# Landings of the GpSimd load queue modelled one microsecond later in a kernel's planner, and a new order of work

## The chip, the cores and the metric

The kernel runs on one core of one Trainium2 chip. The metric is the device time of one execution in microseconds (us); less is better. Eight runs of the kernel before took 263.6, 265.0, 262.32, 261.89, 261.75, 263.05, 262.64 and 262.27 us: the median is 262.48 us.

A core has engines that each work through their own list of instructions in order: TensorE (PE in the profile; it multiplies matrices, and loads weights beside that, PEld), VectorE (DVE), ScalarE (ACT), GpSimd (POOL) and SyncE (SP). They wait for each other by semaphores. Transfers from and to memory (DMA) are issued here by two of them: SP, whose queue is q1, and POOL, whose queue is q0. Both queues are served by the same 16 DMA engines.

## What is computed

Attention over selected blocks, and then a mixer of tokens and of channels on its output. Sizes: 4 batches, 8 heads, 768 positions, 64 values per head; 512 channels, 256 hidden tokens, 1536 hidden channels.

```python
k_rep = k.reshape(B, H, n_blocks, block, D).mean(axis=3)          # blocks of 64 positions
gate_scores = np.einsum('bhsd,bhnd->bhsn', q, k_rep)              # causal blocks only
top_idx = np.argsort(gate_scores, axis=-1)[..., -3:]              # three blocks, and the own one
scores = np.where(mask, q @ k.T / np.sqrt(D), -1e9)
x = softmax(scores) @ v                                           # then heads side by side: 512 channels
h = np.maximum(xt @ w_tok1, 0.0) @ w_tok2                         # xt: x with tokens last
u = x + h.transpose(0, 2, 1)
out = u + np.maximum(u @ w_ch1, 0.0) @ w_ch2
```

## The kernel before

**Work.** Heads are handled in 16 pairs, numbered 0 to 15; four pairs make a batch. For each pair i:

- SP loads k and q (`load_qk`, L453; two halves of 192 KB each; three buffers for k and three for q).
- PE turns them (`transposes`, L498; here "turn k i" and "turn q i", six matmuls each) into a PSUM buffer of the ring "big", which has two buffers; ACT or DVE copies the result out (`evac_t`).
- POOL casts it into the 16-bit arrays KA and QA, one half for each head x (`cast`, L513; "cast k i x").
- PE and DVE find the selected blocks (gate, three largest values, mask).
- PE computes scores (`scores`, L672) in three groups for each head, also into "big"; ACT takes the exponential (L685); DVE masks the diagonal (L692).
- PE multiplies with v ("av i x", L704), and DVE normalises. v of pair i is loaded by POOL's queue (`load_v`, L460; "V i"), into one of six buffers.

For each batch the mixer follows: tok1 (L766 in batch 0, L735 after it), umix (L780, L747), ch1 (L816), ch2 (L833), and the store. Its weights come by POOL's queue in ten loads, W0 to W9: W0 and W1 for tok1 and umix, W2 to W5 for ch1, W6 to W9 for ch2.

**Order.** The kernel writes no order by hand. A planner in the kernel (`plan`) runs when the program is built. It gives every piece of work a cost and a priority, plays the engines forward in its own model, and records the pieces in the order of that model; each engine then executes its pieces in just this order. The priorities are base values plus a table of some 500 small corrections, `NUDGE`, which a search found ("climbed") for the model. Two more tables say after which cast a load on POOL's queue may stand: `VAFTER` for V 0 to V 15 and `WAIT` for W0 to W9 (used at L994 to L1002). They set places in POOL's list, and no waits for data.

In the model of the DMA queues (`transfers`) the queue of POOL and that of SP share a rate, and a load counts as landed some time after its last byte: 1200 ns for POOL's queue, 700 ns for SP's. Where the model sees PE idle in the first 46 us, the planner puts small matmuls on a buffer of zeros there (`dummy`, L850, 55 ns each)[...].

Of the kernel before, what the change touches and what calls it, by code (L numbers as in the profile page):

```python
# [40 lines left out]
def QACT(i):  # L41
# [3 lines left out]
VAFTER = [('kt', 1, 1), ('qt', 3, 1), ('qt', 3, 1), ('qt', 3, 1), ('qt', 4, 1), ('qt', 4, 1), ('kt', 7, 1), ('qt', 8,  # L45
    1), ('qt', 10, 1), ('qt', 12, 1), ('qt', 12, 1), ('qt', 12, 1), ('kt', 13, 1), ('qt', 14, 1), ('kt', 14,
    1), ('kt', 12, 1)]
# [4 lines left out]
WAIT = [('kt', 1, 1), ('kt', 1, 1), ('kt', 3, 1), ('kt', 3, 1), ('qt', 4, 1), ('qt', 4, 1), ('kt', 9, 1), ('qt', 6,  # L52
    1), ('qt', 6, 1), ('qt', 10, 1)]


NUDGE = {('av', 0, 0): 1.303, ('av', 0, 1): 19.19, ('av', 1, 0): 3.0, ('av', 1, 1): 7.0, ('av', 10, 0): 12.27, ('av',
    10, 1): -1.3, ('av', 11, 0): 8.583, ('av', 11, 1): 1.7, ('av', 12, 0): -10.583, ('av', 12, 1): -3.759,
    ('av', 13, 0): -9.736, ('av', 13, 1): -13.215, ('av', 14, 0): 9.3, ('av', 14, 1): -6.4, ('av', 15, 0):
    1.5, ('av', 15, 1): -16.1, ('av', 2, 0): -24.676, ('av', 2, 1): -5.771, ('av', 3, 0): -15.21, ('av', 3,
    1): 14.3, ('av', 4, 0): 0.224, ('av', 4, 1): -15.976, ('av', 5, 0): 9.232, ('av', 5, 1): -3.9, ('av', 6,  # L60
    0): 1.19, ('av', 6, 1): 4.4, ('av', 7, 0): 4.184, ('av', 7, 1): 4.895, ('av', 8, 0): -26.172, ('av', 8,
    1): -1.175, ('av', 9, 0): 4.793, ('av', 9, 1): 20.5, ('bias', 0): -9.3, ('bias', 1): -35.4, ('bias', 2):
    -10.876, ('bias', 3): -28.1, ('bias', 4): 5.3, ('bias', 5): -4.817, ('bias', 6): -24.7, ('bias', 7):
    -12.0, ('bias', 8): 1.624, ('cast', 'kt', 0): 7.5, ('cast', 'kt', 1): -14.6, ('cast', 'kt', 10): -7.747,
    ('cast', 'kt', 11): -15.7, ('cast', 'kt', 12): -14.8, ('cast', 'kt', 13): -12.198, ('cast', 'kt', 14):
    -6.8, ('cast', 'kt', 15): -9.29, ('cast', 'kt', 2): 1.0, ('cast', 'kt', 3): 5.0, ('cast', 'kt', 4):
    -13.647, ('cast', 'kt', 5): 18.165, ('cast', 'kt', 6): 33.55, ('cast', 'kt', 7): -14.305, ('cast', 'kt',
    8): 2.4, ('cast', 'kt', 9): 7.4, ('cast', 'qt', 0): 7.252, ('cast', 'qt', 1): 8.4, ('cast', 'qt', 10):
    -8.041, ('cast', 'qt', 11): 5.7, ('cast', 'qt', 12): 1.4, ('cast', 'qt', 13): 7.4, ('cast', 'qt', 14):
    -12.496, ('cast', 'qt', 15): 8.0, ('cast', 'qt', 2): -5.802, ('cast', 'qt', 3): -8.9, ('cast', 'qt', 4):  # L70
    3.916, ('cast', 'qt', 5): 30.7, ('cast', 'qt', 6): -10.2, ('cast', 'qt', 7): 8.8, ('cast', 'qt', 8): -8.4,
    ('cast', 'qt', 9): 1.1, ('ch1', 0, 1): -0.8, ('ch1', 0, 2): 3.2, ('ch1', 0, 3): 2.5, ('ch1', 1, 0): -9.2,
    ('ch1', 1, 1): -11.5, ('ch1', 1, 2): 0.7, ('ch1', 1, 3): 0.5, ('ch1', 2, 1): -3.7, ('ch1', 2, 2): -0.9,
    ('ch1', 2, 3): -10.3, ('ch1', 3, 0): -7.3, ('ch1', 3, 1): -0.4, ('ch1', 3, 2): 0.3, ('ch1', 3, 3): -0.3,
    ('dg', 0, 0): -17.2, ('dg', 0, 1): 2.993, ('dg', 1, 0): -2.7, ('dg', 1, 1): -4.7, ('dg', 10, 0): -13.711,
    ('dg', 10, 1): 6.989, ('dg', 11, 0): 6.4, ('dg', 11, 1): -19.8, ('dg', 12, 0): 2.907, ('dg', 12, 1): 6.1,
    ('dg', 13, 0): -0.81, ('dg', 13, 1): 6.8, ('dg', 14, 0): 20.5, ('dg', 14, 1): -11.389, ('dg', 15, 0):
    21.39, ('dg', 15, 1): 2.9, ('dg', 2, 0): 2.145, ('dg', 2, 1): -3.182, ('dg', 3, 0): 9.793, ('dg', 3, 1):
    -0.1, ('dg', 4, 0): 11.12, ('dg', 4, 1): -0.9, ('dg', 5, 0): -5.9, ('dg', 5, 1): -1.348, ('dg', 6, 0):
    9.4, ('dg', 6, 1): 10.7, ('dg', 7, 0): -11.565, ('dg', 7, 1): 6.3, ('dg', 8, 0): 0.2, ('dg', 8, 1):  # L80
    -6.683, ('dg', 9, 0): 8.793, ('dg', 9, 1): 11.1, ('ex', 1, 0): 8.2, ('ex', 1, 1): 1.7, ('ex', 10, 0):
    -12.228, ('ex', 10, 1): 30.172, ('ex', 11, 0): 11.3, ('ex', 11, 1): 5.059, ('ex', 12, 0): 6.8, ('ex', 12,
    1): -6.9, ('ex', 13, 0): 5.202, ('ex', 13, 1): -16.7, ('ex', 14, 0): 19.3, ('ex', 14, 1): 2.2, ('ex', 15,
    0): 19.9, ('ex', 15, 1): 0.422, ('ex', 2, 0): 4.583, ('ex', 2, 1): -5.641, ('ex', 3, 0): 12.596, ('ex', 3,
    1): 18.909, ('ex', 4, 0): 9.424, ('ex', 4, 1): -7.694, ('ex', 5, 0): 5.485, ('ex', 5, 1): -17.7, ('ex', 6,
    0): -24.1, ('ex', 6, 1): 0.6, ('ex', 7, 0): -23.0, ('ex', 7, 1): -6.974, ('ex', 8, 0): -16.166, ('ex', 8,
    1): 9.077, ('ex', 9, 0): 17.89, ('ex', 9, 1): 5.545, ('gate', 0): 17.0, ('gate', 1): -7.9, ('gate', 11):
    -6.1, ('gate', 15): -10.725, ('gate', 2): 6.749, ('gate', 3): -6.2, ('gate', 4): -1.007, ('gate', 5):
    19.769, ('gate', 7): 2.6, ('gm', 0): 46.696, ('gm', 1): 17.1, ('gm', 2): -5.382, ('gm', 3): -4.582, ('gm',
    4): 18.193, ('gm', 5): 6.763, ('gm', 6): 8.191, ('gm', 7): -1.6, ('gm', 8): -4.431, ('kcopy', 0): 8.403,  # L90
    ('kcopy', 1): -13.1, ('kcopy', 10): -0.34, ('kcopy', 11): 6.362, ('kcopy', 12): 12.117, ('kcopy', 13):
    -3.285, ('kcopy', 14): 5.152, ('kcopy', 15): 1.6, ('kcopy', 2): -0.869, ('kcopy', 3): -3.3, ('kcopy', 4):
    -12.187, ('kcopy', 5): 2.0, ('kcopy', 6): 35.9, ('kcopy', 7): 4.195, ('kcopy', 8): -0.043, ('kcopy', 9):
    6.264, ('ksum', 0): 17.593, ('ksum', 1): 11.0, ('ksum', 10): 17.559, ('ksum', 11): 4.7, ('ksum', 12):
    -4.3, ('ksum', 13): -7.9, ('ksum', 14): -3.033, ('ksum', 15): -3.69, ('ksum', 2): 17.048, ('ksum', 3):
    -2.1, ('ksum', 4): 26.3, ('ksum', 5): 12.754, ('ksum', 6): 1.797, ('ksum', 7): 3.6, ('ksum', 8): -54.4,
    ('kt', 0): 3.4, ('kt', 1): 7.0, ('kt', 10): 11.272, ('kt', 11): 0.8, ('kt', 12): 14.2, ('kt', 13): -9.9,
    ('kt', 14): -13.5, ('kt', 15): 10.118, ('kt', 2): 13.818, ('kt', 3): -22.9, ('kt', 4): -12.776, ('kt', 5):
    -11.008, ('kt', 6): -17.826, ('kt', 7): -33.297, ('kt', 8): -20.826, ('kt', 9): 2.028, ('lt', 0): -25.61,
    ('lt', 1): -5.5, ('lt', 2): 9.2, ('lt', 3): -25.3, ('lt', 4): 0.9, ('lt', 5): -2.1, ('lt', 6): 6.0, ('lt',  # L100
    7): -5.5, ('lt', 8): -10.776, ('mask', 0): 14.19, ('mask', 1): 9.1, ('mask', 2): -5.031, ('mask', 3):
    -2.9, ('mask', 4): -3.463, ('mask', 5): 15.502, ('mask', 6): 2.681, ('mask', 7): 8.708, ('mask', 8):
    -34.0, ('norm', 0, 0): 3.203, ('norm', 0, 1): -5.307, ('norm', 1, 0): 1.7, ('norm', 1, 1): 11.8, ('norm',
    10, 0): -2.676, ('norm', 10, 1): -13.641, ('norm', 11, 0): 24.7, ('norm', 11, 1): -17.9, ('norm', 12, 0):
    -19.1, ('norm', 12, 1): -5.0, ('norm', 13, 0): -2.7, ('norm', 13, 1): -12.84, ('norm', 14, 0): 1.337,
    ('norm', 14, 1): -20.9, ('norm', 15, 0): -1.2, ('norm', 15, 1): -19.577, ('norm', 2, 0): 9.823, ('norm',
    2, 1): -49.782, ('norm', 3, 0): -0.1, ('norm', 3, 1): -21.3, ('norm', 4, 0): 13.385, ('norm', 4, 1): -6.8,
    ('norm', 5, 0): 17.905, ('norm', 5, 1): -5.6, ('norm', 6, 0): 12.08, ('norm', 6, 1): -2.7, ('norm', 7, 0):
    5.72, ('norm', 7, 1): 0.2, ('norm', 8, 0): -17.047, ('norm', 8, 1): -19.759, ('norm', 9, 0): -3.855,
    ('norm', 9, 1): 8.6, ('put', 0): -5.51, ('put', 1): -11.9, ('put', 10): -3.841, ('put', 11): -1.8, ('put',  # L110
    12): -13.5, ('put', 13): -11.209, ('put', 14): 6.6, ('put', 15): 11.1, ('put', 2): 4.118, ('put', 3):
    10.7, ('put', 4): -2.9, ('put', 5): 6.805, ('put', 6): -12.923, ('put', 7): -23.98, ('put', 8): -24.414,
    ('put', 9): 6.5, ('qt', 0): -10.7, ('qt', 1): 8.0, ('qt', 10): -9.6, ('qt', 11): 13.6, ('qt', 12): 23.4,
# [43 lines left out]
             norm=3, tok1=3, relu1=3, uput=3, utr=3, umix=4, uadd=4)  # L157
# [32 lines left out]
def transfers(moves):  # L190
# [4 lines left out]
    now, ends = 0.0, {}  # L195
    while todo[True] or todo[False]:
# [13 lines left out]
        for q, (_, o) in head.items():  # L210
            left[id(o)] -= step * rate[q]
            if left[id(o)] <= 1e-6:
                todo[q].pop(0)
                ends[o] = now + (1200 if q else 700)
# [946 lines left out]
```

## Time and profile before

| what | value |
|---|---|
| median of 8 runs | 262.48 us |
| the profiled execution: its time | 263.6 us |
| its span, from the first to the last instruction | 261.9 us |
| matmuls / DVE / ACT / POOL busy | 253.7 / 159.7 / 144.0 / 78.5 us |
| granted TensorE clock | full in the mean |
| V loads: issue to landing, least / median / most | 4.3 / 6.5 / 12.3 us |
| k loads / q loads: median to landing | 5.1 / 5.7 us |
| weight loads: median to landing | 7.4 us (8 for ch1, ch2), 8.0 us (2 for tok1, umix) |

The spans of matmuls overlap in the profile, since they are pipelined: "busy" says that PE had something in flight. How fast it goes is seen from the distance of starts in an unbroken row. A long row of L833 has 52 matmuls of 512 columns in 11.22 us, that is 0.216 us for each.

### The profile page before, as it was taken

To read this page: it belongs to the slowest core of one execution; us is meant where nothing else is said; L and a number is where in the kernel's file an instruction comes from. 1 tells how busy PE (TensorE), PEld (TensorE's weight loads), DVE (VectorE), ACT (ScalarE), POOL (GpSimd) and SP (SyncE) were. 2 spreads that over 40 slices of the span, in tenths; PEclk is the share of its full clock that TensorE was granted. 3 is DMA by queue.
4 is the path that set the end of the run, shared out by engine and by line. 5 is a ranking of instruction groups with operands and counts; after the bars stand their busy time and mean duration, and the time that the engine had idled before them with its cause. 6 is when DMAs were issued, how large, how long until landed. Compare 5 with 4: busy or idle time off the path is not lost.

```text
span 261.9 us, 5873 instructions
## 1 busy us (share of the span) xinstructions
PE 253.7 (97%) x2330; PEld 164.4 (63%) x2330; DVE 159.7 (61%) x544; ACT 144.0 (55%) x195; POOL 78.5 (30%) x112
## 2 busy tenths in 40 slices
PE   8999979999999999999999999999999999999994
PEld 7976767886767686567555666644456544465443
DVE  4579879995897589974789755472233262333222
ACT  2878868788698867878716889610044300044000
POOL 8099609828366836636400000000000000000000
PEclk9999999999999999999999999999999999999999
DMA  8999998999999999099212000008310019210032
GB/s 168 220 174 197 198 196 155 191 203 174 173 183 189 184 199 123 3 190 125 52 40 81 3 0 3 3 0 204 116 43 0 0 47 195 80 40 3 0 147 94
DMA packets 91323, 28.78 MB, mean 110 GB/s; under 512 B 84896, under 2 KB 87840, under 8 KB 91296
## 3 DMA queue, kind: packets, MB, share of 16 engines
q1 hardware_dynamic: 63232, 21.33, 37.7%
q0 software_dynamic: 28064, 7.08, 29.1%
q8 instruction: 18, 0.29, 0.5%
q14 instruction: 9, 0.07, 0.1%
HBM read 26.83 MB, written 6.29 MB: 126 GB/s over the span
## 4 chain that ended last, share of the span: by engine, by line
PE 92%; DMA 3%; POOL 1%; ACT 1%; DVE 1%; issue 0%; DVEq 0%
PE c L816 24%; PE c L833 24%; PE sps L672 12%; PE avp L704 8%; PE tql L498 4%; PE tkl L498 4%; DMA V<-in_v_dram 3%; PE avp L850 3%; PE ups L747 3%; PE tok L735 3%; PE gtp L576 1%; PE bps L652 1%; PE tok L766 1%; PE ups L780 1%; PE gps L555 1%; POOL QA L513 1%
## 5 line engine op out<-in xcount | busy, mean ns | idle before, releaser
L685 ACT ACTIVATE e<-sps 128x1024 f16<-128x1024 f32 (+1 forms) x96 | 84.6, 919 | 13.9 <-PE sps L672 10.9
L816 PE MATMUL c<-uT,wc 128*128 128x256 f16 (+1 forms) x384 | 69.4, 326 | 1.2 <-DVE h L444 1.2
L833 PE MATMUL c<-wc,h 128*128 128x512 f16 (+2 forms) x300 | 66.6, 370 | 0.0
L442 ACT ACTIVATE h<-c 128x512 f16<-128x512 f32 (+1 forms) x47 | 27.5, 585 | 64.4 <-PE c L833 37.8
L816 PEld LDWEIGHTS <-wc 128*128 128x128 f16 x384 | 36.7, 97 | 24.5 <-issue 2.0
L672 PE MATMUL sps<-QA,KA 88*128 88x256 f16 (+3 forms) x256 | 50.3, 305 | 1.0 <-ACT e L685 1.0
L833 PEld LDWEIGHTS <-h 128*128 128x128 f16 x300 | 28.7, 98 | 30.4 <-issue 0.2
L444 DVE TENSOR_SCALAR h<-c 128x256 f16<-128x256 f32 (+1 forms) x49 | 21.8, 445 | 30.0 <-PE c L816 23.2
L672 PEld LDWEIGHTS <-KA 88*128 88x128 f16 x256 | 22.7, 98 | 18.6 <-issue 1.0
L841 DVE TENSOR_TENSOR ob<-u,c 128x512 f32<-128x512 f16 (+2 forms) x25 | 16.5, 663 | 27.1 <-PE c L833 27.1
L692 DVE TENSOR_TENSOR e<-e,m 128x256 f16<-128x256 f16 x90 | 26.7, 308 | 10.0 <-ACT e L685 9.4
L513 POOL CAST KA<-kt 64x768 f16<-64x768 f32 x30 | 24.8, 827 | 25.4 <-ACT kt L436 20.0
L513 POOL CAST QA<-qt 64x768 f16<-64x768 f32 x30 | 24.7, 824 | 22.4 <-ACT qt L436 17.1
L704 PEld LDWEIGHTS <-e 128*128 128x128 f16 x672 | 25.3, 97 | 3.9 <-issue 1.3
L704 PE MATMUL avp<-V,e 128*128 128x65 f16 x672 | 26.5, 193 | 1.2 <-DMA V<-in_v_dram 1.2
L526 DVE TENSOR_REDUCE kst<-kt 128x12 f32<-128x768 f32 x16 | 15.0, 948 | 6.1 <-ACT kt L436 6.0
L723 DVE TENSOR_TENSOR x<-avp,rc 128x384 f16<-128x384 f32 x32 | 17.8, 555 | 0.7
L436 ACT COPY kt<-tkl 128x768 f32<-128x768 f32 x16 | 12.6, 800 | 9.7 <-PE tkl L498 7.9
L460 POOL DMA_DIRECT2D V<-in_v_dram x16 | 16.4, 1029 | 0.0
L755 DVE TENSOR_TENSOR u<-x,ups 128x512 f16<-128x512 f16 x18 | 11.9, 683 | 5.1 <-PE ups L747 5.0
L436 ACT COPY qt<-tql 128x768 f32<-128x768 f32 x15 | 12.0, 801 | 5.4 <-PE tql L498 5.2
L658 DVE COPY QA<-bps 24x640 f16<-24x640 f16 x32 | 14.4, 481 | 0.6 <-PE bps L652 0.2
(76 smaller groups left out, 215.4 us busy)
## 6 DMA issues: line engine op xcount, KB each, us to landing
kl<-in_k_dram SPq DMA_DIRECT2D x32, 192.0 KB, 5.1
ql<-in_q_dram SPq DMA_DIRECT2D x32, 192.0 KB, 5.7
out_dram<-ob SPq DMA_DIRECT2D x23, 256.0 KB, 2.0
V<-in_v_dram POOLq DMA_DIRECT2D x16, 192.0 KB, 6.5
wc<-in_moe_w_ch_dram POOLq DMA_DIRECT2D x8, 384.0 KB, 7.4
w<-in_moe_w_tok_dram POOLq DMA_DIRECT2D x2, 384.0 KB, 8.0
out_dram<-ob SPq DMA_DIRECT2D x1, 160.0 KB, 1.8
out_dram<-ob SPq DMA_DIRECT2D x1, 96.0 KB, 1.7
```

The costliest lines, as they stand in the source:

```text
L436: nc.scalar.copy(out=out, in_=in_)
L442: nc.scalar.activation(out=out, in_=in_, func=AF.Relu)
L444: nc.vector.tensor_scalar(out=out, in0=in_, scalar1=0.0, scalar2=None, op0=ALU.max)
L498: nc.tensor.transpose(out=p[:, 128 * j:128 * j + 128], in_=t[:, j, :], identity=ident32)
L513: nc.gpsimd.tensor_copy(out=to, in_=src)
L672: nc.tensor.matmul(out=p[:, off + a:off + a + n], lhsT=KA[i % R][x][0:MK, 128 * kk:128 * kk + 128], rhs=QA[i % R][x][0:MK, q0 + a:q0 + a + ...
L685: nc.scalar.activation(out=e[:, 0:width], in_=T["sps", i, x, g][:, 0:width], func=AF.Exp, scale=scale)
L692: nc.vector.tensor_tensor(out=d, in0=d, in1=m0.rearrange("p (a b) -> p a b", a=1).broadcast_to([128, 2, 128]), op=ALU.mult)
L704: nc.tensor.matmul(out=p[:, jq, :], lhsT=T["e", i, x, g][:, o:o + 128], rhs=V16[i % (R + 1)][:, x, kk, :], start=(kk == 0), stop=(kk == jq))
L723: nc.vector.tensor_tensor(out=T["x16", b][:, :, 64 * hh:64 * hh + 64], in0=T["aps", i, x][:, :, 0:64], in1=T["rc", i, x].broadcast_to([128 ...
L816: nc.tensor.matmul(out=p, lhsT=wc1_16[:, cc, 128 * fc:128 * fc + 128], rhs=T["uT", b][:, cc, a // 128:e // 128, :], start=(cc == 0), stop= ...
L833: nc.tensor.matmul(out=T["c2", b, j, lo], lhsT=T["h2", b][:, fc, 128 * j:128 * j + 128], rhs=wc2_16[:, fc, lo:hi], start=(fc == 0), stop=( ...
```

## The change

Four things in the planner's input, none in the functions that issue instructions: the landing of POOL's loads in the model, the two tables of places, and the table of corrections, which were searched anew with the later landing.

```diff
@@ tables @@
-VAFTER = [('kt', 1, 1), ('qt', 3, 1), ('qt', 3, 1), ('qt', 3, 1), ('qt', 4, 1), ('qt', 4, 1), ('kt', 7, 1), ('qt', 8,
-    1), ('qt', 10, 1), ('qt', 12, 1), ('qt', 12, 1), ('qt', 12, 1), ('kt', 13, 1), ('qt', 14, 1), ('kt', 14,
-    1), ('kt', 12, 1)]
+VAFTER = [('kt', 1, 1), ('qt', 3, 1), ('qt', 2, 1), ('qt', 3, 1), ('kt', 2, 1), ('qt', 5, 1), ('kt', 6, 1), ('qt', 7,
+    1), ('kt', 12, 1), ('kt', 12, 1), ('qt', 12, 1), ('kt', 13, 1), ('qt', 12, 1), ('qt', 12, 1), ('qt', 15,
+    1), ('qt', 15, 1)]
...
-WAIT = [('kt', 1, 1), ('kt', 1, 1), ('kt', 3, 1), ('kt', 3, 1), ('qt', 4, 1), ('qt', 4, 1), ('kt', 9, 1), ('qt', 6,
-    1), ('qt', 6, 1), ('qt', 10, 1)]
+WAIT = [('kt', 1, 1), ('qt', 1, 1), ('kt', 4, 1), ('kt', 5, 1), ('kt', 3, 1), ('kt', 4, 1), ('qt', 9, 1), ('kt', 7,
+    1), ('kt', 8, 1), ('kt', 11, 1)]
...
@@ transfers @@
-                ends[o] = now + (1200 if q else 700)
+                ends[o] = now + (2200 if q else 700)
```

`NUDGE` is replaced from one end to the other. What comes out is another order of the same pieces. Counted in the built programs, every group of matmuls has as many members as before, but for the dummies (122, now 121); eleven relus of ch1 move between ACT and DVE, in total three more on ACT.

POOL's list up to W3 (c k 2 stands for both casts of k 2; a third number is the head):

```
before: c k1, c q1 0, V0, c q1 1, c q2, c k2, W0, W1, c q3, c k3 0, V1 V2 V3, c k3 1, W2 W3, c k4, c q4, W4 W5, own masks, V4 V5
after:  c k1, c q1 0, V0, c q1 1, W0, W1, c k2, c q2 0, c q3, c q2 1, V1 V2 V3, c k3 0, c k4, c k3 1, W2 W4 W5, V4, c q4, own masks, c k5, W3
```

PE's list from the start to av 2 0 (d: dummies; in parentheses the pieces of a stretch):

```
before: ... turn q3 (with 9 d, scores 0 1 2, 9 d ahead of it), mask 1, turn k3, av 0 0, ..., av 0 1, ..., av 1 0, ..., av 1 1, turn k4, turn q4, av 2 0
after:  ... turn q3, 7 d, scores 0 1 1, 4 d, scores 0 1 2, mask 1, 6 d, turn k3, scores 1 0 0, 4 d, av 0 0, ..., turn k4, ..., av 0 1, ..., av 1 0, ..., av 1 1, ..., turn q4, ..., av 2 0
```

PE's list at the end of the loads of k and q:

```
before: tok1 1 0, turn k14, mask 7, turn q14, tok1 1 1, ...   (turn q15 and turn k15 stand some 20 us later, ahead of av 10 0)
after:  tok1 1 0, turn k12, turn q13, tok1 1 1, turn q12, turn k14, umix 1 0, umix 1 5, turn q14, turn q15, umix 1 1, umix 1 2, turn k15, mask 7
```

SP's list has k and q of pair 0 to 15 in the same order in both. The wait that the built program puts on the load of q 15 (its buffer must be free) is for the last matmul of tok1 1 1 after the change, and before it for a piece of ch1 that stands ahead of turn k12. From the second half of batch 1 on, ch1 and the scores of pairs 12 to 15 are mixed in another way, and from the ch2 of batch 1 to the end the lists are the same but for places within ch1 and umix.

## The prediction

> **What bounds the kernel now.** I read the page's first two parts, then PE's waits, then the timelines of POOL and PE.
>
> ```profile
> PE 253.7 (97%) x2330; PEld 164.4 (63%) x2330; DVE 159.7 (61%) x544; ACT 144.0 (55%) x195; POOL 78.5 (30%) x112
> ...
> DMA  8999998999999999099212000008310019210032
> ```
>
> PE has work in flight nearly all the time, and no other engine comes near. The DMA row: each digit is 6.5 us, so for the first 100 us the 16 engines are full too. Up to there PE lives on what has just landed.
>
> ```profile
> PE avp L704 <- DMA V<-in_v_dram: 1.2, 1, 1.2
> PE c L816 <- DVE h L444: 1.2, 2, 0.6
> PE sps L672 <- ACT e L685: 1.0, 3, 0.5
> ```
>
> These are all of PE's recorded waits but the start's. To find time that these rows don't show, I added up PE's list at the pitches of the trace (distance of starts in unbroken rows: 21 of av in 0.67 us, 6 transposes in 0.67, a group of scores 0.44 or 0.27, 4 matmuls of 512 columns 0.87, a dummy 0.055) and compared with real starts. PE **lags** that sum by 3.5 us at av 0 0 (22.96), 6.7 at av 1 0 (34.36), 7.2 at av 2 0, 7.9 at the first ch1 (59.72), 8.3 at tok1 1 0 (97.75), about 9.5 at the end. So 3.2 us go between av 0 0 and av 1 0, little after.
>
> The change keeps every matmul and drops one dummy (0.055 us). Nothing becomes faster by itself: the time can move only by the lag. Head, tail and the two 0.6 us waits at ch1 of batches 2 and 3 lie in lists that stay alike: 0.
>
> **Part 1: W0 and W1 ahead of four casts.**
>
> ```profile
> 20.97 0.82 POOL L861 DMA_DIRECT2D w<-in_moe_w_tok_dram  x1
> ...
> 25.36 3.06 POOL L460 DMA_DIRECT2D V<-in_v_dram  x3
> ...
> 34.36 0.82 PE L704 MATMUL avp<-V,e 128*128 128x65 f16 x21 [1.22 <-DMA V<-in_v_dram]
> ```
>
> av 1 0 is ready at 33.15 and waits for V1, issued at 25.36, landed 9.0 us later. Ahead of it in the queue: V0 (landed 22.7), W0 (28.3), W1 (30.5). W0 landed 5.6 us after V0, being issued only when V0 was nearly in: the queue ran empty for about 1.4 us (a W takes some 2 us under load by the next gaps; 2 to 4 us for W0 leave 1.4 as a middle; ends 0 and 2.6). After the change W0 follows the cast of q1 1, that is at 17.6 instead of 20.97, so the gap closes; V1 to V3 are issued at about 24 (behind the same seven casts of 0.83). V1 then lands at 34.4 − 1.4 = 33.0. Is PE there? Its sum to av 1 0 is 27.5 (before 27.7), but ACT sets the pace, since scores wait for the exponential that frees their buffer: from the first exponential of head 0 1 at 18.97, eight of 0.93, two of 0.61, three copies of 0.75 and one of 0.25 make 11.2, ACT's gaps about 0.9, and scores 1 1 2 with a umix follow, which brings av 1 0 to 31.8. So V1 is still last: wait about 1.2, over at 33.0. **Gain 1.4.** V2, V3 land 2.5 us apart, needed at 37.1 and 41: covered. turn q3, now earlier (19.2), finds q3 landed at 18.3; the dummies round it move with it and cover ACT's pace as before.
>
> Here a rule and the rows part. The Trainium skill (DMA: Bandwidth & Descriptors, "Anatomy of one DMA — SWDGE (gpsimd) path") gives a fixed 2.0 us and bytes / 436e3 for a load by this queue: an estimate of 2.5 us for V's 192 KB. The trace:
>
> ```profile
> DMA to landing us min/median/max: 9.0/10.8/12.3
> ```
>
> That is V1 to V3; V9 and later, with little beside them, take 4.3 to 4.9. Landings differ by contention, not by a constant, which speaks against a constant microsecond in the model: too little at 25 us, too much at 100. By the rule V1 would be in at 27 and the gain 2.6 (34.4 − 31.8). I take the rows.
>
> **Part 2: W2 W4 W5 V4, and W3 after c k5.** V4 is issued at 33 instead of 44.7 (landed 54.3 then, just ahead of av 4 0 at 54.48), needed at about 50.5: behind V3 (38), three W of 2 us and itself it lands at 47 to 48. 0. W3 stands behind c k5: PE's sum at the end of turn k5 is 39.5, copy 0.8, casts 1.7, so W3 goes out at sum 42.0 and ch1 needs it at 49.5: 7.5 us of cover against 4.9 and 6.5 us to landing (W4, W5). 0; if uncovered (W0, W1 took 7.3 and 8.7), up to 1.2. SP's loads: k8 is needed at 56.4 with the lag, landed at 57.3 before, but V5 no longer stands in the queue ahead; q8 goes out as av 4 1 starts (sum 47.7) and is needed at 53.5: 5.8 us against 3.8 to 4.6 unloaded. 0, ends 0 and 1.0.
>
> **Part 3: turn q15 and turn k15 brought forward by 20 us.** In sum time tok1 1 1 ends at 90.9. Only then is q15 issued: the built program waits for that matmul. Behind tok1 1 1 PE has turn q12, turn k14, two umix, turn q14 = 3 × 0.67 + 2 × 0.43 = 2.9 us, then turn q15. PE runs in order, so everything queues behind it: scores of pair 8, ch2 of batch 0, all after.
>
> ```profile
> L453 SPq DMA_DIRECT2D ql<-in_q_dram x2: 491/549/607, 95.9 to 96.4; - x2
> DMA to landing us min/median/max: 3.8/4.0/4.1
> ```
>
> Before, q15 was issued at 95.9 and its second half at 96.4, which landed 4.1 us later: 4.6 in all, hidden by 20 us. Now 4.6 − 2.9 = 1.7 are bare. The quietest row (q12: 0.5 + 3.6 = 4.1) leaves 1.2; V8, issued some 0.6 us behind q15, shares the engines. By the same section's formula (given for POOL's kind of queue), half a load is 2.0 + 0.45, with 0.5 for the second half 2.95: the wait would all but vanish. The rows of this very load decide: **cost 1.6**, ends 0 and 5 (q14, which met W9 and V8, took 5.8 and 8.3).
>
> **Part 4: the rest of the way.** Behind it, DVE has four rows of maxima, lt, bias, six uadd (0.68) and eight mask copies (0.45) before scores 8 0 0 finds its mask; by their sum it is ready 0.1 us late, the second umix bank 0.1 to 0.4. turn k15 holds one of the two "big" buffers until c k13 1 is done, so the scores of pair 8 run on one: scores 8 0 1 stands 1.25 us behind the end of 8 0 0, whose exponential takes 1.0. I take **0.3** for all of it, ends 0 and 1.0. V8 to V15 are issued 6 us or more ahead of their av: hidden by ch2 and ch1. Three more relus on ACT (0.6 each) fall where ACT is 80% busy: 0. From scores 14 0 0 to 15 1 2 ACT needs 10 us in 12: 0.
>
> **Sum.** −1.4 + 1.6 + 0.3 = +0.5 us. The profiled execution would go from span 261.9 (time 263.6, 1.7 around it) to 262.4; on the median of 262.48 it is **263.0**. About 0.5% (1.3 us) is what can be told from no change, so this is "same".
>
> **Rivals.**
> - *q15 lands late* (slower). Place: turn q15. If V8, V9 share with it as W9 and V8 did with q14, it takes 6.0 us, bare 3.1: −1.4 + 3.1 + 0.3 = +2.0, **264.5**. It decides from a landing of 5.3 us on. For: POOL issues V8, V9 right then. Against: V9 did the same 1.7 us behind q15 before.
> - *W3 or q8 late* (slower): +1.2 at the first ch1 or turn q8, and the rest as forecast: +1.7, **264.2**. Against: POOL's queue is empty at that time.
> - *The load is in time* (faster): landing in 2.95 us, as the formula has it: −1.4 + 0.3 = −1.1; with V1 at the gap's far end −2.6 + 1.6·(0 to 1) + 0.3, **261.0**. For: q15 is alone on SP's queue. Against: no q or k row below 3.0 for one half.
> - *The order changes nothing*: V1 isn't earlier since SP's loads take the freed share, and the load hides: ±0, **262.5**.
>
> **Numbers.** Forecast (own range 261.5 to 263.8) 0.33; nothing moves 0.06; q15 late 0.24; W3 or q8 late, or several tight places of part 4 at their ends, 0.16; in time 0.21. From the parts' ends the low is 261.0 and the high 265.5. Faster by over 0.5% 0.21, within 0.39, slower 0.40.
>
> **What would show it.** PE's waits after: one for V at av 1 0 ending near 33, and a new one at L498 for ql with some 1.6 us at about 102. Lag at av 1 0 5.4, at tok1 1 0 about 7, behind turn q15 about 8.5. Wrong if V1 lands no earlier, if PE waits at the first ch1 or at turn q8, or if a wait of over 0.5 us stands behind 110 us that was not there before.

## The result and the profile after

The changed kernel takes 264.2 us (median of 11 runs, 263.59 to 264.9), the kernel before, run beside it on the same chip, 262.69 us (32 runs): the ratio is **1.0052, 95% interval 1.0032 to 1.0073**, about 1.4 us slower. The forecast was 263.0 in a range of 261.0 to 265.5 (for its own case alone 261.5 to 263.8). A second set of runs of the same kernel (below) gave 1.0028 (1.0010 to 1.0046), so one or two thousandths are not to be told apart here.

The page of the changed kernel, first busy row and DMA row:

```profile
PE 253.3 (96%) x2329; PEld 163.1 (62%) x2329; DVE 161.4 (61%) x541; ACT 146.8 (56%) x198; POOL 79.3 (30%) x112
...
DMA  8999999969998979966542000008310019210032
```

PE has one matmul less, the dummy. DVE has 541 instructions instead of 544, and ACT three more: small as it is, that difference comes back below. PE's waits (engine, line, tile, what it waited for: total, times, longest; one of 0.2 us is left out) in the profiled execution, whose span is 263.3 us:

```profile
PE tkl L499 <- DMA kl<-in_k_dram: 1.4, 1, 1.4
PE avp L851 <- DVE warm L1100: 1.3, 1, 1.3
PE c L817 <- DVE h L445: 1.1, 2, 0.6
PE sps L673 <- ACT e L686: 0.7, 1, 0.7
PE avp L705 <- DVE e L693: 0.6, 1, 0.6
PE tql L499 <- issue: 0.4, 1, 0.4
PE bps L653 <- DVE bn L643: 0.3, 1, 0.3
```

The wait for V is gone. In its place stand a wait for k2 in the first 14 us, one at turn q15 (tql), one for an exponential's mask on DVE (avp, L705) and one for the maxima's bias (bps, L653). Where they lie:

```profile
13.94 0.85 PE L499 MATMUL tkl<-id,kl 128*128 128x128 f32 x6 [1.36 <-DMA kl<-in_k_dram]
...
33.28 0.83 PE L705 MATMUL avp<-V,e 128*128 128x65 f16 x21
...
71.33 0.47 PE L653 MATMUL bps<-id,bn 128*64 128x128 f16 x5 [0.30 <-DVE bn L643]
...
102.33 0.84 PE L499 MATMUL tql<-id,ql 128*128 128x128 f32 x6 [0.41 <-issue]
...
113.11 0.69 PE L705 MATMUL avp<-V,e 128*128 128x65 f16 x16 [0.63 <-DVE e L693]
```

The first lies in a part of PE's and SP's lists that is the same before and after. The row at turn q15 names no releaser ("issue": nothing that the profile shows), but in all four profiles in which turn q15 has this place it starts 0.09 us after the second half of q15 has landed, so the wait is for that load.

To compare the rest, I take the prediction's lag (real start minus the sum of PE's list at its pitches) and subtract the lag at av 0 0, so that what a single execution lost in its first 23 us drops out. Other pitches move a whole row by up to 1 us, but the differences within a row by 0.1 only. In us, one profile each:

| lag since av 0 0, at | before (second profile) | changed (second profile) | changed + 3 memsets | before, W early | changed, q15 later | changed, DVE edit | changed, both edits |
|---|---|---|---|---|---|---|---|
| av 1 0 | 2.96 | 1.41 | 1.45 | 1.76 | 1.41 | 1.42 | 1.40 |
| first ch1 of batch 0 | 4.21 | 2.52 | 2.55 | 3.51 | 2.53 | 2.52 | 2.52 |
| tok1 1 0 | 4.54 | 3.71 | 3.77 | 3.84 | 3.69 | 3.69 | 3.71 |
| scores 8 0 0 | 4.47 | 4.32 | 3.71 | 3.76 | 3.73 | 3.87 | 3.75 |
| av 9 0 | 4.65 | 5.34 | 4.73 | 3.94 | 4.57 | 4.09 | 3.81 |
| first ch1 of batch 3 | 5.64 | 6.16 | 5.56 | 4.94 | 5.40 | 4.92 | 4.64 |

The first profiles of both kernels give the same within 0.2. So the changed kernel gains 1.6 to 1.7 us by the first ch1, still has 0.8 of it at tok1 1 0, and has given all of it back by av 9 0.

### The profile page after: what moved, and what is told of

Same layout as the page of the kernel before. It is cut to its first block, busy times and chain, and to the rows that moved or that the text cites. A ratio compares the mean times of both kernels' runs of the same rounds, so it can differ in the third digit from the quotient of the medians.

```text
span 263.3 us, 5856 instructions
## 1 busy us (share of the span) xinstructions
PE 253.3 (96%) x2329; PEld 163.1 (62%) x2329; DVE 161.4 (61%) x541; ACT 146.8 (56%) x198; POOL 79.3 (30%) x112
## 4 chain that ended last, share of the span: by engine, by line
PE 86%; DVE 6%; SPq 2%; DMA 2%; issue 1%; ACT 0%; DVEq 0%; ACTq 0%
PE c L817 23%; PE c L834 22%; PE sps L673 13%; PE avp L705 8%; PE tkl L499 4%; PE tql L499 3%; PE tok L736 3%; PE ups L748 3%; DMA kl<-in_k_dram 2%; SPq L454 2%; DVE QA L659 2%; PE gtp L577 1%; PE tok L767 1%; PE bps L653 1%; PE ups L781 1%
## 5 line engine op out<-in xcount | busy, mean ns | idle before, releaser
L443 ACT ACTIVATE h<-c 128x512 f16<-128x512 f32 (+1 forms) x50 | 29.2, 586 | 59.5 <-PE c L817 22.9
L673 PE MATMUL sps<-QA,KA 88*128 88x512 f16 (+3 forms) x256 | 49.8, 305 | 0.7 <-ACT e L686 0.7
L445 DVE TENSOR_SCALAR h<-c 128x256 f16<-128x256 f32 (+1 forms) x46 | 19.6, 427 | 28.5 <-PE c L817 21.9
L693 DVE TENSOR_TENSOR e<-e,m 128x256 f16<-128x256 f16 x90 | 28.0, 323 | 12.9 <-ACT e L686 12.1
L673 PEld LDWEIGHTS <-KA 88*128 88x128 f16 x256 | 22.0, 97 | 16.7 <-issue 0.9
L705 PEld LDWEIGHTS <-e 128*128 128x128 f16 x672 | 25.5, 98 | 3.9 <-DVE e L693 1.0
L705 PE MATMUL avp<-V,e 128*128 128x65 f16 x672 | 26.9, 193 | 0.8 <-DVE e L693 0.6
L527 DVE TENSOR_REDUCE kst<-kt 128x12 f32<-128x768 f32 x16 | 15.2, 948 | 6.2 <-ACT kt L437 6.1
L499 PE MATMUL tkl<-id,kl 128*128 128x128 f32 x96 | 13.5, 277 | 1.4 <-DMA kl<-in_k_dram 1.4
```

Of the source, the lines that this page charges most:

```text
L443: nc.scalar.activation(out=out, in_=in_, func=AF.Relu)
L445: nc.vector.tensor_scalar(out=out, in0=in_, scalar1=0.0, scalar2=None, op0=ALU.max)
L499: nc.tensor.transpose(out=p[:, 128 * j:128 * j + 128], in_=t[:, j, :], identity=ident32)
L673: nc.tensor.matmul(out=p[:, off + a:off + a + n], lhsT=KA[i % R][x][0:MK, 128 * kk:128 * kk + 128], rhs=QA[i % R][x][0:MK, q0 + a:q0 + a + ...
L693: nc.vector.tensor_tensor(out=d, in0=d, in1=m0.rearrange("p (a b) -> p a b", a=1).broadcast_to([128, 2, 128]), op=ALU.mult)
L705: nc.tensor.matmul(out=p[:, jq, :], lhsT=T["e", i, x, g][:, o:o + 128], rhs=V16[i % (R + 1)][:, x, kk, :], start=(kk == 0), stop=(kk == jq))
```

## Experiments

The theory: the gain is W0 and W1 alone, and it is eaten by new stalls behind it that add up. The rivals: the stalls hide each other; or the constant itself is what matters. Each edit below moves named operations in the finished order; `shift(names, anchor)` takes them out and puts them behind the anchor.

**W0 and W1 alone** (before):

```diff
     order, span = plan(ops, RINGS)
+    shift(["W0", "W1"], "cast_qt_1_1")
```

> The kernel before with one edit: W0 and W1 are put in POOL's list right behind the second half of the cast of q1, where the changed kernel has them; everything else keeps its order. If the gap in POOL's queue ahead of W0 is what makes V1 late (part 1 of the prediction), W0 goes out near 17 instead of 20.97, V1 lands near 32 to 33 instead of 34.4, the wait for V at av 1 0 shrinks from 1.2 us or goes, and the time falls by 1.0 to 1.7 us (ratio 0.9935 to 0.996). Rival: SP's loads take the freed share or the stalls lie in series, so that the next late thing (exponentials, the W of batch 0) takes the place: the time falls by less than 0.5 us (ratio above 0.998).

Measured: 0.9966 (0.9945 to 0.9987), 0.9 us faster. POOL's rows in its trace:

```profile
16.55 0.82 POOL L861 DMA_DIRECT2D w<-in_moe_w_tok_dram  x1
...
24.48 3.06 POOL L460 DMA_DIRECT2D V<-in_v_dram  x3
```

W0 goes out at 16.55 instead of 20.97, V1 is in before av 1 0 at 32.11, and no wait for V is left. The lag at av 1 0 falls by 1.2, of which 0.5 returns by the first ch1. So two loads are most of the changed kernel's gain at av 1 0 (1.2 of 1.55) but less than half of it at the first ch1 (0.7 of 1.7): the theory holds for the start alone. From there on the 0.7 is kept to the end, where the changed order loses its larger gain.

**Both new stalls taken out of the changed kernel:**

```diff
     order, span = plan(ops, RINGS)
+    shift(["tr_ql_15", "qt_15"], "mask_7")
+    shift(["ksum_14", "kcopy_12"], "dg_8_0_2")
```

> The changed kernel with two edits: turn q15 and its copy stand behind the mask of group 7 on PE and in the pools' order (later than the landing of q15), and on DVE the sum of k14 and the copy of k12 stand behind the diagonal of av 8 0. If the two new stalls behind tok1 1 1 are what the change pays (theory: 0.4 at turn q15, 0.6 at av 8 0), both waits are gone and the time is 0.8 to 1.1 us under the changed kernel, about that of the kernel before (ratio 0.999 to 1.002). Rival: the tight place is DVE's sum of work round pair 8, so that what is moved out of it is late at the next place, and the time stays within 0.3 us of the changed kernel (ratio 1.004 to 1.006).

Measured: 0.9998 (0.9984 to 1.0012); the unchanged copy beside it 1.0028. Both waits are gone, and the lag at av 9 0 is 3.81 instead of 5.34. The time falls by 0.8 us, at the low end of what the theory had.

**The two edits singly.**

> The changed kernel with one edit: on DVE the sum of k14 and the copy of k12 stand behind the diagonal of av 8 0. Theory (the two stalls behind tok1 1 1 add up): turn q15 still waits 0.4 to 0.8 us, the wait at av 8 0 (0.6, lag +0.8) goes, the lag from av 0 0 to the last ch1 falls from 6.2 to 5.4 and the time by 0.6 to 0.8 us against the changed kernel (ratio to before 1.000 to 1.002). Rival (what DVE puts off is late at the next place, the exponential or the diagonal of av 8 1): the lag at av 9 0 stays above 5.1 as without the edit, ratio 1.003 to 1.005.

> The changed kernel with one edit: turn q15 and its copy stand behind the mask of group 7. Theory (the stalls add up): the wait at turn q15 is gone or below 0.2 us, av 8 0 still waits 0.6, lag at av 9 0 falls by 0.5 to 0.7 and the ratio to before is 1.000 to 1.002. Rival (the stalls hide each other: DVE's sum of work sets when av 8 0 can start, whatever PE lost before): the wait at av 8 0 grows to 1.1 to 1.4, the lag at av 9 0 stays within 0.2 of the changed kernel's, ratio 1.003 to 1.005.

DVE's edit: 1.0020 (1.0007 to 1.0034). The later turn: 1.0028 (1.0016 to 1.0041), above its expected ratio. Neither interval is clear of the unchanged copy's 1.0028 (1.0010 to 1.0046), so the times do not tell what one edit is worth. The traces do. DVE in the changed kernel, ahead of av 8 0:

```profile
110.43 0.50 DVE L659 COPY QA<-bps 24x640 f16<-24x640 f16 x1
110.94 0.95 DVE L527 TENSOR_REDUCE kst<-kt 128x12 f32<-128x768 f32 x1
111.81 0.32 DVE L535 TENSOR_REDUCE ks<-kst 64x12 f32<-64x12 f32 x2
112.17 0.69 DVE L842 TENSOR_TENSOR ob<-u,c 128x512 f32<-128x512 f16 x1
112.77 0.28 DVE L693 TENSOR_TENSOR e<-e,m 128x256 f16<-128x256 f16 x1
```

The mask product at L693, which av 8 0 waits for, stands behind k14's sum (0.95) and a copy, neither of which is needed yet. With DVE's edit it comes first:

```profile
109.23 0.69 DVE L842 TENSOR_TENSOR ob<-u,c 128x512 f32<-128x512 f16 x1
109.84 0.36 DVE L693 TENSOR_TENSOR e<-e,m 128x256 f16<-128x256 f16 x1
110.13 0.94 DVE L527 TENSOR_REDUCE kst<-kt 128x12 f32<-128x768 f32 x1
```

and the wait is gone, with nothing late behind it. With the later turn alone, PE still waits at av 8 0:

```profile
111.20 0.68 PE L705 MATMUL avp<-V,e 128*128 128x65 f16 x16 [0.60 <-DVE e L693]
```

0.60 and not 1.1 to 1.4, so the stalls don't hide each other: in lag they add. The stall at turn q15 is the less steady one: 0.56, 0.72, 0.29 and 0.03 of lag in the four profiles that keep its place, with landings of the second half after 4.0, 4.2, 3.7 and 3.5 us. That the later turn's median shows no gain fits a stall that is worth 0.4 us on the average, below what these intervals tell.

**The same two kernels again.**

> The changed kernel without an edit, for a second profile. In its first profile PE waited 1.36 us for k2 at turn k2 (12.6 to 13.9 us) and the last stores took 0.5 us longer, in parts of the lists that are the same before and after. If that is chance of one execution, this profile shows the start's lag as in the kernel before (lag about 3.0 us at the first mask instead of 3.9), while the waits at turn q15 (0.4) and av 8 0 (0.6) are there again. If it belongs to the change, the wait for k2 of over 1 us is there again. The ratio is 1.005 either way.

> The kernel before without an edit, for a second profile. If the start's wait for k2 is chance, it can show up here too, or a start without it; the wait for V at av 1 0 (1.2 us) and the two waits at ch1 of batches 2 and 3 (0.6) are there again, and no wait at turn q15 or av 8 0.

The changed kernel: 1.0028; its second profile has no wait for k2 (lag at the first mask 2.0), and the waits at turn q15 and av 8 0 are back:

```profile
PE avp L705 <- DVE e L693: 0.6, 1, 0.6
PE tql L499 <- issue: 0.6, 1, 0.6
```

The kernel before waited 1.0 us for V at av 1 0 this time, 0.6 twice at ch1, and at neither of the two other places. The wait for k2 is thus of the execution, not of the change: of the seven profiles of the changed order this first one alone has it. Other short waits for a first load turned up in kernels of either order: 0.2 to 0.6 us at turn k0, some 5 us into the span, in four profiles.

**The constant alone, and the table alone.**

```diff
-                ends[o] = now + (1200 if q else 700)
+                ends[o] = now + (2200 if q else 700)
```

> The kernel before with the planner's landing constant alone at 2200, and the old table of offsets and old load positions: the whole order is planned anew from offsets that were climbed on the other constant. Theory (the table only fits the model that it was climbed on): new waits turn up in several places and the time is 1 to 5 us above before (ratio 1.004 to 1.02). Rival (the constant alone brings the good part, since landings of this queue take 4 us and more in the trace): the time falls by 0.5 us or more (ratio below 0.998).

> The changed kernel with the constant put back to 1200 and the new table and load positions: planned anew. By the same theory 1 to 5 us above the changed kernel (ratio to before 1.008 to 1.025); rival, the constant matters little once the table is there: within 0.5 us of the changed kernel (ratio 1.002 to 1.006).

1.0134 (1.0098 to 1.0171) with the old table and the new constant, 1.0123 (1.0098 to 1.0148) the other way round. PE's waits in the first of them:

```profile
PE avp L704 <- DMA V<-in_v_dram: 2.0, 2, 1.4
PE tql L498 <- DMA ql<-in_q_dram: 1.8, 2, 1.6
```

Its V4 is still issued at 44.0 us and is late at av 4 0 (the longest wait for V, 1.4 us), and q8 is late at its turn (1.6 us). Offsets that were climbed on one model cost over 1% on the other here; the constant on its own isn't an improvement.

**The end of the kernel.** The lag explains 0.5 us between the second profiles, and the stores at the end another part. The DMA view from the issue of the last store but one to the end (queues: packets, MB, share; issues: KB, us to landing), first before, then changed:

```profile
q1 hardware_dynamic: 362, 0.38, 33.6%
issues: line engine op xcount, KB each, median us to landing
out_dram<-ob SPq DMA_DIRECT2D x1, 160.0 KB, 1.8
out_dram<-ob SPq DMA_DIRECT2D x1, 96.0 KB, 1.7
```

```profile
q1 hardware_dynamic: 363, 0.38, 29.5%
q14 instruction: 1, 0.01, 0.9%
issues: line engine op xcount, KB each, median us to landing
out_dram<-ob SPq DMA_DIRECT2D x1, 160.0 KB, 2.3
out_dram<-ob SPq DMA_DIRECT2D x1, 96.0 KB, 2.1
```

A packet of the instruction queue (8 KB) falls between the last stores, and packets of theirs come after it. From the issue of the last store but one to the end of the span it is 3.2 us in the profiles without that packet, 3.5 to 3.8 in the six that have it: 0.3 to 0.6 us more, 0.4 on the average. Which engine's code is it? DVE's list is three shorter. So: three idle memsets on DVE in the changed kernel, and, the other way round, three memsets of the start moved from DVE to POOL in the kernel before.

```diff
         nc.vector.memset(m0, 1.0)
+        for _ in range(3):
+            nc.vector.memset(pad, 0.0)
```

> The changed kernel with one edit: three small memsets on DVE at the start, into a tile that nothing reads, so that DVE has as many instructions as in the kernel before (the changed planner gave three relus of DVE's to ACT). In every profile so far of a kernel with the shorter DVE list (five) an 8 KB packet of the instruction queue starts 0.6 to 0.9 us behind the issue of the last store but one, and that store and the last take 2.2 to 2.5 and 2.0 to 2.3 us; in the five with the longer list the packet is 3.7 us ahead of that issue and the stores take 1.8 and 1.7. Theory (the length of DVE's list places this packet): it is back at 3.7 us ahead, the stores take 1.8 and 1.7, the time falls by 0.3 to 0.5 us (ratio to before 1.001 to 1.004). Rival (the late stores come of something else in the order): packet and stores stay as in the changed kernel.

```diff
         for t in g1 + [gt]:
-            nc.vector.memset(t[:, 0:64], 0.0)
+            nc.gpsimd.memset(t[:, 0:64], 0.0)
```

> The kernel before with one edit: three memsets of the start (the two gate buffers and their transposed one) on POOL instead of DVE, so that DVE's list is three shorter, as in the changed kernel; the order of everything planned is as before. Theory of the instruction packet: it falls 0.6 to 0.9 us behind the issue of the last store but one, the last two stores take 2.2 and 2.0 us or more instead of 1.8 and 1.7, and the time rises by 0.3 to 0.5 us (ratio 1.000 to 1.003). Rival: packet and stores stay as before.

The changed kernel with three memsets, in the same view of its end:

```profile
q1 hardware_dynamic: 363, 0.38, 34.2%
issues: line engine op xcount, KB each, median us to landing
out_dram<-ob SPq DMA_DIRECT2D x1, 160.0 KB, 1.8
out_dram<-ob SPq DMA_DIRECT2D x1, 96.0 KB, 1.7
```

The kernel before with three fewer on DVE:

```profile
q14 instruction: 1, 0.01, 1.0%
issues: line engine op xcount, KB each, median us to landing
out_dram<-ob SPq DMA_DIRECT2D x1, 160.0 KB, 2.1
out_dram<-ob SPq DMA_DIRECT2D x1, 96.0 KB, 2.0
```

The packet and the late stores go and come together with DVE's count of instructions, in both directions. The two replanned kernels, with 542, have stores of 1.8 and 1.7 us. The ratios, 1.0018 (1.0002 to 1.0034) and 1.0005 (0.9985 to 1.0025), agree with 0.3 us but are too wide to show it by themselves.

**A version that beats both.** Both kernels have two waits of 0.6 us at the start of ch1 in batches 2 and 3 ("PE c <- DVE h"). The first relu of the batch waits 18.89 us, to the very end of the last ch2 of the batch before, because the hidden tile has one buffer; its first third is read only by the first third of that ch2. So the tile is cut in three:

```diff
-            if fc == 0 and ("h2", b) not in T:
-                T["h2", b] = sb("h2", [128, NFC, S], F16, f"h2_{b}")
-            relu(eng, T["h2", b][:, fc, a:e], T["c1", b, fc, n])
+            if ("h2", b, fc // 4) not in T:
+                T["h2", b, fc // 4] = sp.tile([128, 4, S], F16, tag=f"h2{fc // 4}", bufs=1, name=f"h2_{b}_{fc // 4}")
+            relu(eng, T["h2", b, fc // 4][:, fc % 4, a:e], T["c1", b, fc, n])
```

(and ch2 reads the third that belongs to its part), once on the kernel before with W0 and W1 early, once on the changed kernel with both edits and the memsets.

> The kernel before with W0 and W1 early (as in the first experiment) and the hidden tile of the channel part cut in three by its 12 slices, so that the first relu of batches 2 and 3 waits only for the first of the three parts of the last ch2, not for all of them. If the two waits at ch1 of batches 2 and 3 (0.6 us each, lag +0.75 each) come of this one buffer, both are gone and the time is 1.2 to 1.5 us under the first experiment's, that is 2.0 to 2.5 us under before (ratio 0.990 to 0.9925). Rival (PE's banks or the adds of ch2 hold ch1 back anyway): both waits stay, ratio 0.995 to 0.998.

> The changed kernel with all the edits: turn q15 later, the sum of k14 and the copy of k12 behind the diagonal of av 8 0, the three memsets, and the hidden tile in three. By the lags (after the start: 4.6 us instead of the 5.7 of before, then 1.5 less by the cut tile) it ends with b_best: ratio 0.990 to 0.994. Rival (the changed kernel's start is later for a reason that the profiles don't show, since its three-to-one run of medians lies 0.6 us above what its lags give): 0.5 us or more above b_best.

Measured: **0.9922 (0.9899 to 0.9946)**, 260.86 us, and **0.9913 (0.9890 to 0.9937)**, 260.66 us. The relu in the W-early kernel without the cut, and with it:

```profile
189.01 0.60 ACT L442 ACTIVATE h<-c 128x512 f16<-128x512 f32 x1 [18.89 <-PE c L833]
```

```profile
187.11 0.60 ACT L442 ACTIVATE h<-c 128x512 f16<-128x512 f32 x1 [16.67 <-PE c L816]
```

It now follows its own ch1 (L816) and not the last ch2 (L833), and both waits are gone. The cut alone was not run; from W early (0.9966) to W early with the cut (0.9922) it is 1.2 us. The two versions end level, in time as in lag since av 0 0 at the first ch1 of batch 3 (4.06 and 4.00): once its new stalls are out, the changed order is no better than the old one with two loads moved. The rival of a start that is later for a hidden reason is not borne out.

## Why the prediction came out as it did

The time lay in the forecast's outer range, above the 261.5 to 263.8 of its own case, and on the slower side, to which it gave 0.40. That +0.5 us came near is in part luck: it is a sum of terms of which several were off in opposite directions. And one of its signs of being wrong came: a new wait of over 0.5 us behind 110 us (0.63 at 113.11).

- **Part 1: the gain held, what limits it did not.** Forecast: V1 in at 33.0 and still last, a wait of 1.2, gain 1.4. In the first profile W0 went out at 16.89, V1 was issued at 24.17 and landed 7.9 us later at 32.1, and av 1 0 started at 33.28 without a wait for V; in the second it was 31.2 and 31.73. So PE's own pace set av 1 0, and no longer V1. The gain is 1.6 to 1.7 at the first ch1. The row decided rightly against the fixed landing: V1 to V4 took 7.9 to 14.6 us here.
- **Part 2: loads right, stage incomplete.** V4 landed at 47.3 (forecast 47 to 48), W3 6.7 us after its issue, q8 in time: each 0, as said. But of the 1.7 at the first ch1 only 0.8 is left at tok1 1 0. PE waits at the mask of group 6 (0.30 us, about 0.4 of lag), for a bias that stands behind two relus on DVE:

```profile
69.52 0.74 DVE L445 TENSOR_SCALAR h<-c 128x256 f16<-128x256 f32 x2
70.18 1.09 DVE L643 SCALAR_TENSOR_TENSOR bn<-gm,gown 128x120 f16<-128x120 f32 x2
```

  The prediction looked at loads alone in this stretch and did not name it. The other 0.5 is no wait in PE's rows. In part it comes of the comparison: a gate that the old order has done before the first ch1 (51.03 us) comes behind it in the new one (59.92). No run took this stall out by itself.
- **Part 3: the term that was mis-sized.** Forecast: q15 is issued when tok1 1 1 ends, 1.7 us bare, cost 1.6. The trace:

```profile
96.98 0.82 PE L499 MATMUL tql<-id,ql 128*128 128x128 f32 x6
97.64 1.46 PE L736 MATMUL tok<-x,w 128*128 128x512 f16 x6
...
97.83 0.96 SPq L454 DMA_DIRECT2D ql<-in_q_dram  x2
```

  q15 goes out at 97.83, just behind the start of tok1 1 1 (97.64), which ends only at 98.94. In all seven profiles of the changed order its issue comes 0.19 us after tok1 1 1 starts, so the load waits for what stands ahead of it, turn q13 in the list, and not for tok1 1 1 as was read from the built program. The landing was about right (3.9 to 4.6 us in all, forecast 4.6), the release was taken one piece too late, and turn q15 is ready 3.9 us behind the issue and not 2.9. Measured: 0.03 to 0.72, on the average 0.4.
- **Part 4: too little.** Forecast 0.3, with an end of 1.0; measured 0.95: 0.15 at a umix and 0.80 at av 8 0, and DVE's edit takes the latter away. The place named was scores 8 0 0 and its mask; the stall was one step on, at the mask product on DVE.
- **Three relus on ACT: "0".** No new wait for ACT stands in PE's rows, but they made DVE's list three shorter, which put a code packet among the last stores: 0.4 us on the average.

In sum −1.7 + 0.9 + 0.4 + 0.95 = +0.55, less 0.2 that the old order loses later and the new one doesn't, + 0.4 at the end: about +0.75, against measured +0.7 (1.0028) to +1.4 (1.0052). What lies between these two is not settled. The lag at av 0 0 ran from 2.8 to 4.3 in profiles of the changed order and from 2.7 to 3.5 in those of the old; part of it are landings of the first k and q, part a wait of about 0.3 us for DVE at scores 1 0 0 that only some executions of the changed order show.

The rival "q15 lands late" gave 264.5, near the time, but for a wrong reason: q15 landed as usual, and the time went to DVE and the end. The rival by which the load's formula makes q15 free was nearer for this term (0 against a measured 0.4), but also for a wrong reason: the load took its 3.9 us and more, and was issued earlier. The range of 261.0 to 265.5 is not the sum of the parts' ends, which would reach from −2.6 to about +7 us; the forecast doesn't say how it was narrowed.

## What to carry to other kernels

When a planner gives a whole new order, look for the two or three moves that carry the gain and try them on the old order: here two loads moved gave 0.9 us, and the rest of the new order cost more than that. When loads are checked for a new order, the lists of the other engines should be checked too: most of the stalls that the new order brought (0.4 at the mask of group 6, 0.8 at av 8 0) arose on DVE, where a small operation that PE needed stood behind larger ones that could wait. And a wait for a whole buffer that is read in parts (18.89 us behind one tile, 0.6 us of PE twice) can be worth more than reordering: cutting the tile gave some 1.2 us here, the two moved loads 0.9.

## What the hardware showed that was not expected

The number of instructions on DVE moved a code load. With 544 instructions in DVE's row the 8 KB packet was clear of the last two stores; with 541 it fell between them, and they landed in 2.3 and 2.1 us instead of 1.8 and 1.7. Three memsets that do nothing removed it, and three taken from DVE in the other kernel brought it about. The Trainium skill (Runtime: NRT & Kernel Launch, "Instruction fetch mechanics") calls the cost of fetching the next block of instructions mostly hidden (it speaks of blocks of 16 KiB); the packet that met the last stores was not hidden here, and no run measures the others.

A load of V by POOL's queue took 7.9 to 14.6 us from issue to landing at 24 to 33 us into the changed kernel, and the second half of q15 by SP's queue 3.5 to 4.2 us at one place of one order. The first is much the same in every profile of that order (V1 7.0 to 8.0 us, V4 14.2 to 15.2) and can be planned for by the place; the second differs from execution to execution, and half a microsecond of cover decides whether PE sees it.
